# Attention, Sinkhorn gate and eight experts on one core: the opening reordered with the mask formed by GpSimd, and expert 1's leftover pieces dealt out over four slots

## The chip, the core and the metric

The kernel runs on one NeuronCore of a Trainium2 chip. A core has five engines that run their own instruction streams side by side: TensorE (PE in the profile; its weight loads are PEld), VectorE (DVE), ScalarE (ACT), GpSimd (POOL) and SyncE (SP). DMAs are issued from the streams of POOL, ACT and SP and move data on their own; an engine waits for another, or for a DMA, by semaphores. The metric is the device time of one execution in microseconds (us), as the median of several runs.

## The reference

Global-local attention over 8 batches and 8 heads of width 64, with 512 local and 32 global tokens per batch, and then a mixture of experts over the 8 x 544 = 4352 tokens of width 512. Cut to what matters:

```python
# attention, scale = 1/sqrt(64)
k_all, v_all = concat(k_g, k_l), concat(v_g, v_l)
out_g = softmax(scale * q_g @ k_all.T) @ v_all               # global queries see all
mask  = abs(pos[:, None] - pos[None, :]) <= 32               # local ones a band, and the globals
s_ll  = where(mask, scale * q_l @ k_l.T, -1e9)
out_l = softmax(concat(scale * q_l @ k_g.T, s_ll)) @ concat(v_g, v_l)
x = concat(out_g, out_l) as [4352, 512]
# gate: eight Sinkhorn iterations over a [4352, 8] matrix
P = exp(x @ w_gate - max)
for _ in range(8):
    P /= P.sum(1) + 1e-9;  P /= P.sum(0) + 1e-9;  P *= 4352 / 8
# eight dense experts, every token through each
out = sum over e of P[:, e] * (relu(x @ w1[e]) @ w2[e])      # w1 512x1024, w2 1024x512
```

## The kernel before

All engines' orders are the order in which the program is written: the schedule is manual, and every engine takes its instructions strictly in that order. So a line that is moved in the program moves on every engine that it issues to.

**Opening (L226 to L262).** The first two heads of q and k of batch 0 come as float32 by SP and ACT (L229-231) into a buffer f and are cast by L469. The other six heads come by POOL, four loads for q and four for k (`load_qk`, L149, issued at L161). The mask is a tile of 128 partitions x 3 variants x 160 columns (128 of keys, 32 of globals), added to the scores. Its band is made in DRAM: a row with zeros in its first 65 places and -8e9 behind them (`toep_m`, L142; memsets L232-233) is written out 64 times (`scr_m`, L234) and read back skewed, with a pitch of 255, into the two halves of the middle variant (L240-242); L473-476 copy it to the first and last variants, whose edges they set. Global keys and queries of batches 0 to 3 come as float32 (`load_gf`, L201, issued at L205: keys by ACT, queries by SP behind the mask's reads), are cast on DVE by `cast_g` (L208, L210) and turned by `transpose_g` (L213: PE at L217, DVE copy at L219). Those of batches 4 to 7 are loaded by POOL in slot 6 (`load_g`, L194, issued at L198) and turned at the end of slot 8. `load_v` (L170) loads values: on POOL the global ones to a DRAM copy vg16 (L176), the local ones to va (L177, L180) and a tail of vb (L183), and on SP three copies va to vb, shifted by half a tile (L184-186), which wait for va. `load_vz` (L166, issued at L168) has SP read vg16 into four zero-padded places of vgz. For batch 0 it is called at L548, in slot 0 of the loop. `clear` (L250) sets zeros and ones of the value tiles, for batch 0 on DVE and for batch 1 on POOL.

**Attention loop (L477).** 35 slots s, of which 32 hold a pair of heads each (four slots to a batch). A pair passes through stages in successive slots: `st_A` (L266) turns q and k by PE into PSUM, copies the keys to kTe (L274, DVE) and the queries to qbd (L277, ACT); `st_B` (L279) makes scores (L292, L294), adds the mask and takes the row minimum (L299, DVE) and the exponential (L302, ACT), in three parts; `st_D1` (L305) copies the global part (L308, `Pl`) and turns the rest; `st_D2` (L315) turns more; `st_E` (L332) multiplies by the values va, vb (L343) and vgz (L345). Every second slot `st_G0` (L357) copies two blocks of turned global queries into qgbd (L362, DVE, a pair of copies), and `st_G1` to `st_G4` do the global queries' attention. From slot 6 on, pieces of expert 0 and then 1 are set between these stages: `p_l1` (L429, PE at L436) for the first layer, `p_l2` (L443, PE at L450) for the second. POOL's loads are queued by the slot (L477 ff.); from slot 10 on `sums_load` (L98, issued at L101 or L103) and `sums_form` (L105; four subtractions and additions at L116, result stored at L117) make sums of the later experts' weights on POOL. The gate follows (L423 for the logits, then lines L574 to L626), covered by remaining pieces, the `tail`.

**Experts 2 to 7 (L628 on).** They go by a Strassen-like scheme of seven products. `Slot` (L815) is a quarter of one first-layer tile with products m1 to m7 (PE at L838; copies and relu on ACT and DVE at L849 to L877), `Unit` (L724; PE at L743) the second layer. `token_sum` (L672, DVE at L682) makes the token sums that m6, m7 and m4 read. `run_slot` (L883) sets the order of a slot, with `fill` (L892) inserting leftover pieces of expert 1 while no `Unit` is there. `tail` is a list of (cost, piece); when the experts begin four pieces of expert 1 are left, two `p_l1` and two `p_l2`, and all four are placed in slot 0. `jobs` (L948 ff.) hang weight fetches, loads of stored results (`stored_load`) and their additions (`stored_add`) on slots; a load is issued by the addition three before it.

Of the kernel before, what the change touches and what calls it, by code (L numbers as in the profile page):

```python
# [11 lines left out]
FP32 = mybir.dt.float32  # L12
AF = mybir.ActivationFunctionType
ALU = mybir.AluOpType
# [4 lines left out]
NEG = -8.0e9  # L19
# [4 lines left out]
def kernel(  # L24
# [13 lines left out]
    nc = tc.nc  # L38

    B, H, Sl, Dh = q_l.shape  # L40
# [82 lines left out]
    with ExitStack() as att:  # L123
# [15 lines left out]
        vab = [(att_c.tile([P, NJ, H, VW], FP16, name=f"va{i}"),  # L139
                att_c.tile([P, NJ, H, VW], FP16, name=f"vb{i}")) for i in range(2)]  # L140
        xgn = [att_c.tile([P, D], FP16, name=f"xgn{i}") for i in range(2)]
        LT = 256  # L142
        toep_m = att_wk.tile([HB, LT], FP32, tag="ms")
        scr_m = dscr.tile([HB * LT], FP32)
        vg16 = [dscr.tile([Sg, H, Dh], FP16, name=f"vg16_{b}") for b in range(B)]

        staged = {}
# [73 lines left out]
        def run(steps):  # L221
            for f in steps:
                f()
# [5 lines left out]
        for h in range(2):  # L229
            for t, (src, eng) in enumerate(((q_l, nc.sync), (k_l, nc.scalar))):  # L230
                eng.dma_start(out=fh[t][:, :, h, :], in_=src[0, h].rearrange("(s p) d -> p s d", p=P))
        nc.vector.memset(toep_m, NEG)  # L232
        nc.vector.memset(toep_m[:, 0 : 2 * W + 1], 0.0)
        nc.sync.dma_start(out=scr_m.rearrange("(p l) -> p l", l=LT), in_=toep_m)  # L234
        load_gf(0, "kgs", f0[:, 2, :], (nc.scalar,) * 4)
        run(load_qk(0, 2, H))
        nc.vector.memset(ones_f, 1.0)
        nc.scalar.activation(out=ones_f[:, 0:1], in_=ones_f[:, 0:1], func=AF.Exp, scale=0.0)
        nc.vector.memset(mask[:, :, KW:SW], 0.0)
        for hf in range(2):  # L240
            nc.sync.dma_start(out=mask[HB * hf : HB * (hf + 1), 1, 0:KW],
                              in_=scr_m[0 : HB * (LT - 1)].rearrange("(p l) -> p l", l=LT - 1)[:, 0:KW])
        load_gf(0, "qgs", f0[:, 3, :], (nc.sync,) * 4)
        for t in qbd:
            nc.vector.memset(t, 0.0)
        for t in kTe:
# [11 lines left out]
            eng.memset(qgbd[i], 0.0)  # L258

        clear(0, nc.vector)  # L260
        run(load_v(0))
        clear(1, nc.gpsimd)  # L262

        st = {}
# [1 line left out]
        def st_A(n):  # L266
            b, hp = divmod(n, HP)
            qs, ks = staged[b]
            qb, kt = qbd[n % 2], kTe[n % 4]
            pt = ps_tr.tile([P, 2, Sl], FP16, tag="tr")  # L270
            for t, src in enumerate((ks, qs)):
                for so in range(NJ):
                    nc.tensor.transpose(pt[:, t, P * so : P * (so + 1)], src[:, so, 2 * hp : 2 * hp + 2, :], identity)  # L273
            nc.vector.tensor_copy(out=kt[:, W : W + Sl], in_=pt[:, 0, :])  # L274
            for a in range(2):
                r = slice(HB * a, HB * (a + 1))
                nc.scalar.copy(out=qb[r, :, HB * a : HB * (a + 1)], in_=pt[r, 1, :].rearrange("p (i q) -> p i q", q=HB))  # L277
# [189 lines left out]
        NU = B * HP  # L467
        for t in range(2):
            (nc.vector.tensor_copy if t else nc.scalar.copy)(out=staged[0][t][:, :, 0:2, :], in_=fh[t])  # L469
        cast_g("kgs")  # L470
        st_A(0)
        transpose_g(0, "kgs")
        nc.vector.tensor_copy(out=mask[:, 0, 0:KW], in_=mask[:, 1, 0:KW])  # L473
        nc.vector.tensor_copy(out=mask[:, 2, 0:KW], in_=mask[:, 1, 0:KW])
# [2 lines left out]
        for s in range(NU + 3):  # L477
# [57 lines left out]
            f2("a")  # L535
            if g_odd:
                st_G2(gb, gg)
            if 1 <= s:
                st_D2(s - 1 if s <= NU else None, s - 3 if s >= 3 else None)
            if s < NU:  # L540
                st_B(s, 1)
            if 2 <= s < NU + 2 and even:
                st_E(s - 2, 0)
# [1 line left out]
            if s + 1 < NU:  # L545
                st_A(s + 1)
            if s == 0:
                load_vz(0)  # L548
                cast_g("qgs")
                transpose_g(0, "qgs")  # L550
            if s == 1:
# [81 lines left out]
    with tc.tile_pool(name="tpool", bufs=2) as tpool, \  # L633
# [249 lines left out]
        def run_slot(a, jobs=()):  # L883
            p, x = state["slot"], state["unit"]
            y = units.pop(0) if units else None

            def do(who, *what):
                for w in what:
                    if who is not None:
                        getattr(who, w)()  # L890

            def fill(w):  # L892
                while a is not None and tail and w > 0:
                    w -= tail[0][0]
                    tail.pop(0)[1](pool=ps_z, tag="z")

            do(a, "m1")
            if x is None:
                fill(1)
            do(x, "m4", "m5", "r2", "r7")  # L900
            do(a, "m2")
            do(p, "m4", "m3")
            do(y, "sums", "m1")
            if y is None:
                fill(1)
            do(a, "m6")
            do(x, "m3", "r1")
            do(a, "m5")
            if y is None:
                fill(1)  # L910
            do(y, "m7", "m2", "m6")
            do(a, "m7")
            for j in jobs:
                j()
            do(a, "c22")
            state["slot"], state["unit"] = a, y
# [30 lines left out]
        for k, (pas, e) in enumerate(stages):  # L947
            more = k + 1 < len(stages)  # L948
            slots = ([(NQ, 0)] if pas else []) + [(2 * pas + j, f) for j in range(2) for f in range(HF)]
            jobs = [[] for _ in slots]  # L950
            n = len(slots)
            if more:
                jobs[0 if k else 4].append(lambda: fetch(k + 1, 0))
                jobs[5].append(lambda: fetch(k + 1, 1))
            else:
                jobs[5].append(lambda: work.__setitem__("last", load_w2(e)))
            if e == 2 and pas:
                for i in range(4):
                    jobs[1 + i].append(lambda i=i: token_sum(3, i))
            if e == E - 1 and not pas:  # L960
                for i in range(4):
                    jobs[4 + i].append(lambda i=i: token_sum(2, i))
                    jobs[4 + i].append(lambda i=i: token_sum(NQ, i))
            if e == 2:
                us = [(m, c) for q in (([NQ] if pas else []) + [2 * pas, 2 * pas + 1])
                      for m, c1, c2 in ([(B, 0, 1)] if q == NQ else [(2 * q + i, cc, 2 + cc) for i in range(2) for cc in range(2)])
                      for c in (c1, c2)]
                jobs[2].append(lambda us=us: (yq.extend((ee, m, c) for u in range(0, len(us), 2) for ee in range(2)
                                                        for m, c in us[u : u + 2]),
                                              [stored_load() for _ in range(3)]))  # L970
            for i in range(n):
                if e == 2 and i > 4 or e == 3 and i < 5:
                    jobs[i] += [stored_add, stored_add]
                elif 2 < e < E - 1:
                    jobs[i].append(stored_add)
            for (q, f), js in zip(slots, jobs):
                if k == 0 and q == 1 and f == 0:
                    hset.append([hpool.tile([P, FT, 512], FP16, tag="hT", name="hs") for _ in range(2)])
                run_slot(Slot(k, q, f, hset[q % 2] if q < NQ else hg), js)
                if q == NQ or f == HF - 1:  # L980
                    push(k, q)
# [34 lines left out]
```

## Time and profile before

| | |
|---|---|
| median of 3 runs | 1042.97 us (1042.85 to 1044.25) |
| the profiled execution | 1043.23 us, of which the span of its records is 1041.4 |
| mean granted clock of TensorE | 0.998 |
| PE busy | 997.6 us, 96% of the span |
| DVE, ACT, POOL busy | 808.3 (78%), 652.0 (63%), 292.3 (28%) |
| instructions | 20377 |
| opening, the first two of forty slices of 26 us | PE busy 4 and 7 tenths |

The profile comes from one execution. Its page has the busy time of each engine, the span in 40 slices with a busy digit for each engine, the chain of work that ended last, followed back from the end, and the costliest groups of instructions. The trace behind it answers narrower questions: a timeline lists instructions as start, duration, engine, line, operation, output<-input, and in brackets the idle time just before and what ended it; "x2" joins two of a kind in a row, and the duration is then that of both. A list of waits gives, by engine and line, what was waited for: total, times, longest. A row of windows gives a stretch, its length, then busy time (and count) of PE, PEld, DVE, ACT and POOL, the granted clock, the share of the DMA engines and GB/s. Landing of a DMA means the time at which its completion was signalled.

### The profile page before, as it was taken

What the parts mean: (1) busy time and instruction counts of PE and PEld (TensorE: products, weight loads), DVE (VectorE), ACT (ScalarE), POOL (GpSimd) and SP (SyncE); (2) the same over time, 40 slices, a digit from 0 to 9 for tenths busy, and PEclk for the clock granted to TensorE, in tenths of its full rate; (3) what the DMA queues carried; (4) which work ended last, traced back from release to release, by engine and by line L of the source; (5) the groups of instructions that cost most, each with busy time, mean ns of one, the idle gap of its engine ahead of it and who ended that gap; (6) DMA issues with size and microseconds to landing.
All of it is one profiled execution on the core that took longest, in us unless ns stands there. A gap on an engine that the chain in (4) does not pass through costs nothing.

```text
span 1041.4 us, 20377 instructions
## 1 busy us (share of the span) xinstructions
PE 997.6 (96%) x7786; PEld 656.3 (63%) x7786; DVE 808.3 (78%) x2025; ACT 652.0 (63%) x1377; POOL 292.3 (28%) x309
## 2 busy tenths in 40 slices
PE   4789999999999998999999999999999999999998
PEld 3666666566665454666666666676767676676764
DVE  6786766677765554779999888898789999888885
ACT  5787778777785446775555555556765555555551
POOL 9556665656545422002111111111111111011000
PEclk9999999999999999999999999999999999999999
DMA  9999999999975689255463433456554433333043
GB/s 150 183 161 163 184 186 178 166 177 184 183 165 162 182 211 243 62 152 128 110 135 87 112 65 86 90 165 172 154 119 102 108 103 90 68 71 72 1 102 122
DMA packets 184274, 139.42 MB, mean 134 GB/s; under 512 B 120240, under 2 KB 157552, under 8 KB 180592
## 3 DMA queue, kind: packets, MB, share of 16 engines
q0 software_dynamic: 151904, 87.32, 55.0%
q1 hardware_dynamic: 30128, 50.27, 14.7%
q8 instruction: 61, 1.00, 0.4%
q10 hardware_dynamic: 2144, 0.52, 0.3%
q14 instruction: 37, 0.30, 0.1%
HBM read 144.26 MB, written 39.65 MB: 177 GB/s over the span
## 4 chain that ended last, share of the span: by engine, by line
PE 88%; DVE 5%; DMA 3%; ACT 2%; issue 1%; SPq 0%; DVEq 0%; ACTq 0%
PE z L743 27%; PE pa L838 16%; PE ph L436 11%; PE py L450 10%; PE pb L838 8%; PE pc L838 5%; DMA ys<-yd 2%; PE zp L809 1%; PE sc L292 1%; PE po L343 1%; PE po L345 1%; PE pt L273 1%; PE ptw L311 1%; DVE ms L299 1%; PE sg L372 1%
## 5 line engine op out<-in xcount | busy, mean ns | idle before, releaser
L743 PEld LDWEIGHTS <-hs 128*128 128x128 f16 x2264 | 220.7, 98 | 92.9 <-issue 1.1
L743 PE MATMUL z<-w2e,hs 128*128 128x256 f16 x1304 | 195.6, 273 | 0.9 <-DVE oy L777 0.9
L743 PE MATMUL z<-v,hs 128*128 128x256 f16 x960 | 144.0, 273 | 0.0
L436 PE MATMUL ph<-xT,w1e 128*128 128x512 f16 (+1 forms) x576 | 134.0, 367 | 3.1 <-DVE lg L425 3.1
L450 PE MATMUL py<-w2e,hT 128*128 128x512 f16 x544 | 127.4, 379 | 0.8 <-ACT hT L439 0.8
L838 PEld LDWEIGHTS <-w1e 128*128 128x128 f16 x960 | 86.5, 97 | 61.0 <-issue 4.3
L764 ACT COPY z<-z 128x256 f32<-128x256 f32 x98 | 35.0, 357 | 141.9 <-PE z L743 141.9
L838 PE MATMUL pa<-t,s 128*128 128x512 f16 x384 | 114.2, 379 | 0.8 <-ACT s L863 0.8
L299 DVE CUSTOM_DVE_ANT_0 ms<-sc,mask 128x160 f32<-128x160 f32 x256 | 70.1, 321 | 47.8 <-PE sc L294 46.3
L777 DVE SCALAR_TENSOR_TENSOR oy<-z,lg,oy 128x512 f32<-128x512 f32 x128 | 95.8, 749 | 7.3 <-ACT oy L782 4.4
L739 DVE TENSOR_TENSOR hs<-hs 128x512 f16<-128x512 f16 x224 | 94.8, 423 | 8.1
L302 ACT ACTIVATE Pu<-ms,mx 128x160 f16<-128x160 f32 x256 | 92.2, 426 | 8.2 <-DVE mx L299 6.5
L842 DVE CUSTOM_DVE_ANT_0 hx<-pb,s 128x512 f16<-128x512 f32 x96 | 65.9, 686 | 34.7 <-ACT s L872 28.2
L659 POOL DMA_DIRECT2D w1e<-in_moe_w_dram x24 | 17.4, 730 | 268.5 <-PE pa L838 221.4
L854 ACT ACTIVATE hs<-pc 128x512 f16<-128x512 f32 x96 | 57.2, 596 | 53.7 <-PE pc L838 53.6
L659 POOL DMA_DIRECT2D w2e<-in_moe_w_dram x24 | 19.8, 831 | 241.4 <-PE z L743 238.5
L838 PEld LDWEIGHTS <-s 128*128 128x128 f16 x720 | 65.6, 98 | 34.4 <-issue 6.0
L842 DVE CUSTOM_DVE_ANT_0 hs<-pb,s 128x512 f16<-128x512 f32 x96 | 65.9, 686 | 27.1 <-ACT s L872 26.6
L450 PEld LDWEIGHTS <-hT 128*128 128x128 f16 x544 | 51.2, 98 | 51.8 <-issue 1.2
L436 PEld LDWEIGHTS <-w1e 128*128 128x128 f16 x576 | 52.5, 98 | 45.3 <-issue 3.6
L116 POOL TENSOR_TENSOR psum<-pw 128x1024 f16<-128x1024 f16 x24 | 50.4, 2117 | 104.8 <-DMA pw<-in_moe_w_dram 104.8
L453 ACT COPY yst<-py 128x512 f32<-128x512 f32 x68 | 39.9, 586 | 54.4 <-PE py L450 51.9
(186 smaller groups left out, 2053.3 us busy)
## 6 DMA issues: line engine op xcount, KB each, us to landing
ys<-yd SPq DMA_DIRECT2D x68, 256.0 KB, 3.2
yd<-yst SPq DMA_DIRECT2D x16, 1024.0 KB, 4.4
pw<-in_moe_w_dram POOLq DMA_DIRECT2D x12, 1024.0 KB, 11.3
kept<-psum POOLq DMA_DIRECT2D x12, 1024.0 KB, 4.7
s<-kept POOLq DMA_DIRECT2D x12, 768.0 KB, 9.4
v<-kept POOLq DMA_DIRECT2D x12, 768.0 KB, 9.1
w1e<-in_moe_w_dram POOLq DMA_DIRECT2D x12, 512.0 KB, 5.4
w2e<-in_moe_w_dram POOLq DMA_DIRECT2D x12, 512.0 KB, 6.3
```

The lines of the kernel that those rows point to most:

```text
L116: nc.gpsimd.tensor_tensor(out=o, in0=x, in1=y, op=op)
L299: nc.vector.tensor_tensor_reduce(out=ms[:, ii, :], in0=sc[:, SW * ii : SW * (ii + 1)], in1=mask[:, mi, :], scale=-scale, scalar=BIG, op0=A ...
L302: nc.scalar.activation(out=d["Pu"][:, i, :], in_=ms[:, ii, :], func=AF.Exp, scale=-1.0, bias=d["mx"][:, i : i + 1])
L436: nc.tensor.matmul(ph[:, 0:n], wts[e][0][:, dk, P * fm : P * (fm + 1)], xT[:, dk, c0 : c0 + n], start=(dk == 0), stop=(dk == DP - 1))
L450: nc.tensor.matmul(py, hT[:, fk, P * c : P * (c + 1)], wts[e][1][:, fk, :], start=(fk == 0), stop=(fk == FT - 1))
L453: nc.scalar.copy(out=ys[:, c, :], in_=py)
L739: nc.vector.tensor_tensor(out=o, in0=x, in1=y, op=op)
L743: nc.tensor.matmul(o, lhs[:, fk, :], rhs[:, fk, :], start=(first and fk == 0), stop=(fk == HF - 1), skip_group_check=True)
L777: nc.vector.scalar_tensor_tensor(out=o, in0=z, scalar=p, in1=o, op0=ALU.mult, op1=ALU.add)
L838: nc.tensor.matmul(o, lhs[:, dk, P * f : P * (f + 1)], rhs[:, dk], start=(first and n == 0 and dk == 0), stop=(dk == HD - 1), skip_group_c ...
L842: nc.vector._custom_dve(TENSOR_ADD_SAT, out=self.to(i, j), in0=self.of(ps), in1=self.of(s), s0=BIG, s1=0.0)
L854: nc.scalar.activation(out=self.to(0, 0), in_=self.of(self.pc), func=AF.Relu)
```

## The change

The mask's band is formed in place: the whole mask is zeroed on DVE, and for each half of the partitions two GpSimd selects set -8e9 where the column is left of p or right of p + 64; the row, the DRAM copy and its three DMAs go. The loads of global keys are split between SP and ACT, and those of global queries are issued before `load_qk`'s POOL loads and no longer behind the mask's reads. `load_vz(0)` goes from slot 0 of the loop to just behind the first step of `load_v(0)`, so on SP it stands ahead of the copies va to vb. `st_A(0)` goes ahead of the cast of the global keys. For slots 2 to 6 the copy to kTe is made by ACT. In slots 0 to 6 the second part of the scores goes ahead of `st_D2`. In the expert part `fill` counts pieces rather than cost: `some` is the leftover count divided by the slots left of this quarter, rounded up, so the four leftovers of expert 1 go one to each of the first four slots; and for expert 2 the doubled `stored_add` begins at slot 6 and no longer at slot 5.

```diff
@@ -139,9 +139,6 @@
         vab = [(att_c.tile([P, NJ, H, VW], FP16, name=f"va{i}"),
                 att_c.tile([P, NJ, H, VW], FP16, name=f"vb{i}")) for i in range(2)]
         xgn = [att_c.tile([P, D], FP16, name=f"xgn{i}") for i in range(2)]
-        LT = 256
-        toep_m = att_wk.tile([HB, LT], FP32, tag="ms")
-        scr_m = dscr.tile([HB * LT], FP32)
         vg16 = [dscr.tile([Sg, H, Dh], FP16, name=f"vg16_{b}") for b in range(B)]
 
         staged = {}
@@ -229,18 +226,12 @@
         for h in range(2):
             for t, (src, eng) in enumerate(((q_l, nc.sync), (k_l, nc.scalar))):
                 eng.dma_start(out=fh[t][:, :, h, :], in_=src[0, h].rearrange("(s p) d -> p s d", p=P))
-        nc.vector.memset(toep_m, NEG)
-        nc.vector.memset(toep_m[:, 0 : 2 * W + 1], 0.0)
-        nc.sync.dma_start(out=scr_m.rearrange("(p l) -> p l", l=LT), in_=toep_m)
-        load_gf(0, "kgs", f0[:, 2, :], (nc.scalar,) * 4)
+        load_gf(0, "kgs", f0[:, 2, :], (nc.sync, nc.scalar, nc.sync, nc.scalar))
+        load_gf(0, "qgs", f0[:, 3, :], (nc.sync,) * 4)
         run(load_qk(0, 2, H))
         nc.vector.memset(ones_f, 1.0)
         nc.scalar.activation(out=ones_f[:, 0:1], in_=ones_f[:, 0:1], func=AF.Exp, scale=0.0)
-        nc.vector.memset(mask[:, :, KW:SW], 0.0)
-        for hf in range(2):
-            nc.sync.dma_start(out=mask[HB * hf : HB * (hf + 1), 1, 0:KW],
-                              in_=scr_m[0 : HB * (LT - 1)].rearrange("(p l) -> p l", l=LT - 1)[:, 0:KW])
-        load_gf(0, "qgs", f0[:, 3, :], (nc.sync,) * 4)
+        nc.vector.memset(mask, 0.0)
         for t in qbd:
             nc.vector.memset(t, 0.0)
         for t in kTe:
@@ -258,7 +249,15 @@
             eng.memset(qgbd[i], 0.0)
 
         clear(0, nc.vector)
-        run(load_v(0))
+        for a in range(2):
+            band = mask[HB * a : HB * (a + 1), 1, 0:KW]
+            for base, m, c in ((0, -1, 1), (2 * W, 1, -1)):
+                nc.gpsimd.affine_select(out=band, in_=band, compare_op=ALU.is_ge, fill=NEG, base=base,
+                                        pattern=[[c, KW]], channel_multiplier=m)
+        steps = load_v(0)
+        steps[0]()
+        load_vz(0)
+        run(steps[1:])
         clear(1, nc.gpsimd)
 
         st = {}
@@ -271,7 +270,7 @@
             for t, src in enumerate((ks, qs)):
                 for so in range(NJ):
                     nc.tensor.transpose(pt[:, t, P * so : P * (so + 1)], src[:, so, 2 * hp : 2 * hp + 2, :], identity)
-            nc.vector.tensor_copy(out=kt[:, W : W + Sl], in_=pt[:, 0, :])
+            (nc.scalar.copy if 1 < n < 7 else nc.vector.tensor_copy)(out=kt[:, W : W + Sl], in_=pt[:, 0, :])
             for a in range(2):
                 r = slice(HB * a, HB * (a + 1))
                 nc.scalar.copy(out=qb[r, :, HB * a : HB * (a + 1)], in_=pt[r, 1, :].rearrange("p (i q) -> p i q", q=HB))
@@ -467,8 +466,8 @@
         NU = B * HP
         for t in range(2):
             (nc.vector.tensor_copy if t else nc.scalar.copy)(out=staged[0][t][:, :, 0:2, :], in_=fh[t])
+        st_A(0)
         cast_g("kgs")
-        st_A(0)
         transpose_g(0, "kgs")
         nc.vector.tensor_copy(out=mask[:, 0, 0:KW], in_=mask[:, 1, 0:KW])
         nc.vector.tensor_copy(out=mask[:, 2, 0:KW], in_=mask[:, 1, 0:KW])
@@ -535,9 +534,11 @@
             f2("a")
             if g_odd:
                 st_G2(gb, gg)
+            if s < 7:
+                st_B(s, 1)
             if 1 <= s:
                 st_D2(s - 1 if s <= NU else None, s - 3 if s >= 3 else None)
-            if s < NU:
+            if 7 <= s < NU:
                 st_B(s, 1)
             if 2 <= s < NU + 2 and even:
                 st_E(s - 2, 0)
@@ -545,7 +546,6 @@
             if s + 1 < NU:
                 st_A(s + 1)
             if s == 0:
-                load_vz(0)
                 cast_g("qgs")
                 transpose_g(0, "qgs")
             if s == 1:
@@ -889,25 +889,23 @@
                     if who is not None:
                         getattr(who, w)()
 
-            def fill(w):
-                while a is not None and tail and w > 0:
-                    w -= tail[0][0]
+            def fill(n):
+                for _ in range(min(n, len(tail)) if a is not None else 0):
                     tail.pop(0)[1](pool=ps_z, tag="z")
 
             do(a, "m1")
+            some = -(-len(tail) // (HF - a.f)) if tail and a is not None else 0
             if x is None:
                 fill(1)
             do(x, "m4", "m5", "r2", "r7")
             do(a, "m2")
             do(p, "m4", "m3")
             do(y, "sums", "m1")
-            if y is None:
-                fill(1)
             do(a, "m6")
             do(x, "m3", "r1")
             do(a, "m5")
             if y is None:
-                fill(1)
+                fill(some - 1)
             do(y, "m7", "m2", "m6")
             do(a, "m7")
             for j in jobs:
@@ -969,7 +967,7 @@
                                                         for m, c in us[u : u + 2]),
                                               [stored_load() for _ in range(3)]))
             for i in range(n):
-                if e == 2 and i > 4 or e == 3 and i < 5:
+                if e == 2 and i > 5 or e == 3 and i < 5:
                     jobs[i] += [stored_add, stored_add]
                 elif 2 < e < E - 1:
                     jobs[i].append(stored_add)
```

## Prediction

> **What bounds the kernel now.** I read the page's slices and its chain first.
>
> ```profile
> PE   4789999999999998999999999999999999999998
> DVE  6786766677765554779999888898789999888885
> PE 88%; DVE 5%; DMA 3%; ACT 2%; issue 1%; SPq 0%; DVEq 0%; ACTq 0%
> ```
>
> A slice is 26 us. TensorE (PE) is 90% busy or more from the fourth slice on, and 88% of the chain is PE. Matmuls are only moved by this change, so it can win only where PE waits: in the opening (slices 1 to 3), and where expert 1's leftovers meet expert 2 (393 to 413 us). Second, the waits of PE from 0 to 80 us (columns: total, times, longest) and PE's timeline there.
>
> ```profile
> PE po L345 <- DMA vgz<-vg: 2.9, 2, 2.2
> PE pt L217 <- ACT qbd L277: 0.7, 1, 0.7
> ```
> ```profile
> 28.65 0.27 PE L345 MATMUL po<-vgz,pg 128*128 128x130 f16 x1 [2.18 <-DMA vgz<-vg]
> ...
> 74.19 0.39 PE L217 MATMUL pt<-identity,kgs 128*128 128x128 f16 x4
> 75.30 0.38 PE L217 MATMUL pt<-identity,qgs 128*128 128x128 f16 x4 [0.72 <-ACT qbd L277]
> ```
>
> PE stands 2.9 us for the padded global values, and at 75.30 turns the second half of the global queries, after which it has no gap to 149 us. Third, GpSimd (POOL), which issues nearly all loads: the query load, then batch 3's values and the first weights for its sums.
>
> ```profile
> 68.98 1.14 POOL L198 DMA_DIRECT2D qgs<-in_q_g_dram  x2 [0.45 <-DMA va<-in_v_l_dram]
> ...
> 78.45 0.79 POOL L177 DMA_DIRECT2D va<-in_v_l_dram  x1 [0.74 <-PE po L343]
> 79.23 1.77 POOL L180 DMA_DIRECT2D va<-in_v_l_dram  x2
> 80.97 0.78 POOL L103 DMA_DIRECT2D pw<-in_moe_w_dram  x1
> ```
>
> Before the first of these every wait is for a load that landed, or stands where one did; by the DMA records the last of the four query loads lands at 73.45, 1.85 us ahead of its use. Fourth, PE's waits from 80 to 393 us: the largest row is a wait on VectorE (DVE), gaps of 0.66 us at 149.22 and 2.44 at 192.11. DVE's and POOL's timelines show what DVE did then:
>
> ```profile
> 146.15 2.12 POOL L116 TENSOR_TENSOR psum<-pw,psum 128x1024 f16<-128x1024 f16 x1
> ...
> 188.93 4.20 POOL L116 TENSOR_TENSOR psum<-pw 128x1024 f16<-128x1024 f16 x2 [10.71 <-DMA pw<-in_moe_w_dram]
> ```
> ```profile
> 147.06 1.44 DVE L362 COPY qgbd<-qgT 64x64 f16<-64x64 f16 x2
> ...
> 189.94 3.23 DVE L362 COPY qgbd<-qgT 64x64 f16<-64x64 f16 x2
> ...
> 213.67 0.36 DVE L362 COPY qgbd<-qgT 64x64 f16<-64x64 f16 x2
> ```
>
> Alone (213.67) the pair takes 0.36. Begun inside POOL's L116, it ends as L116 ends: at 193.17 against 193.13, and at 148.50 against 148.27. So at two places DVE, and PE behind it, is held to POOL's clock.
>
> **Part 1, the mask band.** Goes: two memsets (0.27 and 0.11), a write (SP issue 1.79) and two reads of 64 partitions; SP's 3.3 us wait between them goes too. The reads landed by 10.84, the copies L473-474 ended at 11.5 and the first masked reduction ran at 11.74, but PE's next slot waited for the key load ks, landed 13.09. That cover stays; without it the part would give about 1 us at the first reduction. Comes: a memset of 480 columns for one of 96 (0.14), taken as 0.5 by the element count, beside the input loads; and four selects on POOL ahead of the value loads L176-183, hence ahead of every later POOL load. Nearest rows: the identity's select, 0.29 for 128x128 f16, and one L116 operation, 2.1 for 1024 columns, as bounds with below-nothing excluded since POOL runs them in order. I take 0.34 by the first, which has the same columns in half the bytes: 1.35 us in all (1.2 to 8.4).
>
> **Part 2, k_g on both queues, q_g ahead of load_qk.** k_g's cast began at 8.83 and q_g's at 14.38, 0.1 after its landing and behind the kTe copy that ended 14.31; earlier landings meet the same cover, ks at 13.09. Eight issues of 0.5 us leave SP's and ACT's idle first 10 us. Cost nothing; 0.3 either way if ACT's first copies move.
>
> **Part 3, vgz of batch 0.** Its four SP issues (19.64 to 23.53, landed 26.05 to 30.45) go ahead of the copies va to vb, whose waits for va held them. vg landed at 13.65, so issues from 14 to 16.4 and landings by 18, 7 us ahead of PE's use at 25. The waits of 2.9 us go. vb's three copies come later by at most the four issues' 2.4 us where SP was not waiting for va; L186 was issued at 18.95 after va landed 18.23, so they stay nearly where they were. The four loads' 1024 packets also leave POOL's loads alone at 23 to 30 us (a 1024-packet load takes about 0.85 us of landing time in the rows at 75 to 81 us, 1.0 when crowded): POOL's chain regains about 1.0 of its 1.35.
>
> **Parts 4 to 6, order in slots 0 to 6.** Keys ahead of a cast (0.43, under the ks cover); the kTe copy on ScalarE for five slots: 5 x 0.42 off DVE, which is 87 to 96% busy from 30 to 60 us, 5 x 0.59 onto ACT, 73 to 85% busy; scores ahead of a transposition. Between losing 0.9 (ACT's excess) and gaining 2.1. I take 1.0. With part 3 the lead of PE at slot 8 is 3.9 (2.0 to 5.0).
>
> **What then ends last.** Through 18 to 66 us POOL waits for landed loads and not for PE, so the query load cannot follow the lead. It lands at 73.45 + 0.4 (1.35 - 1.0; -0.3 to +1.2), and PE, with 0.1 us for the semaphore, goes on at 73.95: 75.30 - 73.95 leaves **1.35** of 3.9. Then POOL's clock: the values at 78.45 waited for PE until there; now PE releases at 77.1, but POOL, which was free at 77.71, comes at 77.71 + 0.4 = 78.1. So pw is issued 0.35 earlier, and so are L116 and all that POOL does after it, since from here to 225 us POOL waits only for its own weights. The copy pairs at 147 and 189.9, 1 us earlier against L116, still begin inside the row of L116 operations (139.66 to 148.27), or just before one; held to its end, PE leaves at 148.3 with a lead of **0.35** (POOL's bounds: +1.0 to -0.45). A lead beyond POOL's is given back here.
>
> **Part 7, leftovers of expert 1.** Slots 0 to 3 took 6.69, 4.52, 4.37 and 4.42, 20.0 in all, with the four pieces in slot 0:
>
> ```profile
> 393.45:400.14 6.69, 6.69 (x38) 3.42 (x37) 6.12 (x19) 3.64 (x9) 2.71 (x4) 1.00 0.75 156
> 400.14:404.66 4.52, 3.56 (x17) 1.46 (x16) 1.53 (x3) 3.09 (x6) 2.94 (x4) 1.00 1.00 228
> ```
>
> The second and third numbers are length and PE's busy time: slot 0 has no gap, slots 1 to 3 lose 0.96, 1.03 and 1.08 (row: pa copied to pc by ACT, 0.9 each). One piece per slot covers 2.2 of these 3.1. But in slot 0 PE comes to the first token sums at about 395.3, and DVE finishes them at 396.6 and 396.9 (two of 0.38 from 396.18): 1.3 + 0.13 us, and ACT's 0.45 at m7 and 0.4 elsewhere come on top. 2.3 new against 2.2 gone: **+0.1** (-2.5 if DVE's sums move up, +1.0 if ACT's copies queue).
>
> **Part 8, stored_add one slot later.** The stalls of 1.75 at 452.82 and 755.86 wait for a load issued by an add three earlier; same order, cost nothing; a further 1.75 if the add lands beside another load.
>
> **Sum**, on the profiled execution (1043.23; span 1041.4 and 1.83 around it): 1043.23 - 0.35 + 0.1 = 1042.98. The median of the runs is 0.26 lower: **1042.7**.
>
> **Rivals.** *Lead kept:* DVE's copies slip past L116. At 189.94 the pair began 1.0 us into L116, and 1.35 against 0.35 is a shift of just 1.0; if it slips out, the 2.44 goes as well: 1042.97 - 1.35 - 2.44 + 0.1 = 1039.3. For: that edge. Against: at 147 another L116 lies just ahead (143.95 to 146.08), so the hold takes the lead first. [...]
>
> *Clock drop:* PE now stands some 2.5 us (3.9 - 1.35) before 73.95. At 44 to 46 us PE was busy 0.70 of 2.00, and the granted clock was 0.67 and 0.50 in the next two rows of 2 us. A drop of 3.4 us at half costs up to 1.7. It eats the lead of 1.35 and 0.35 more, by which POOL then waits for PE: 1042.97 + 0.35 + 0.1 = 1043.4. Against: PE was busy right before and after. [...]
>
> *Spread hides all:* DVE's token sums, free of the pieces' copies, are ready when PE comes: the 2.3 falls away and 0.3 more: 1042.7 - 2.6 = 1040.1. Against: the sums began at 396.18 behind the gate's work, which doesn't move.
>
> *Slower, the selects:* each costs t above 1.0 us. POOL is then late by 4t - 1.0, comes to 77.71 with it instead of 78.45, and all L116 with it; at t = 1.2, 3.8 - 0.74 = 3.1 is forced on DVE at 147: 1042.97 + 3.1 + 0.1 = 1046.1. It passes +2.1 from t = 0.96. For: L116's 2.1; against: the 0.29 row.
>
> **How the numbers follow.** Forecast 0.50 (with POOL's +1.0 to -0.45 of lead and the spread's +1.0, 1042.0 to 1044.4), clock drop 0.14, lead kept 0.13, spread 0.12, selects 0.11. What a measurement of this kernel can tell from no change is 0.2%, 2.1 us: 1040.9 to 1045.1. Faster: 0.13 + 0.12 = 0.25; same: 0.50 + 0.14 = 0.64; slower 0.11. The range leaves out the selects (0.11): it runs from 1039.1, the lead kept with 0.2 to spare, to 1045.0, the clock drop (+0.35) with the query load at its late end (0.8 more) and the spread's +1.0.
>
> **What would show it.** Selects near 0.34 each; no vgz wait at 25 to 29 us; PE waiting for qgs at 70 to 74; L116 at 91.4 instead of 91.74; a copy pair near 147 or 190 still ending with L116, with a longer gap of PE behind it; slot 0 near 5.0 with a wait for L682, slots 1 to 3 near 4.7 to 5.2. It is wrong if PE's qgs transposes come before 73.5 (loads followed the lead), or if PE's lead at 200 us is not POOL's.

## The result, and the profile after

The changed kernel takes 1047.36 us (median of 14 runs, 1045.35 to 1051.43) against 1042.94 us for the kernel before (14 runs, 1040.15 to 1046.56); the ratio is 1.0043, 95% interval 1.0029 to 1.0057. It is slower, by 4.4 us, and outside the range of 1039.1 to 1045.0 that was forecast. Timed once more on another chip, with 12 runs against 32, the ratio was 1.0026 (1.0009 to 1.0043). The profiled execution after took 1045.89 us, span 1044.1, against 1043.23 and 1041.4 before; it is the second shortest of its 14, so what follows explains less than the whole 4.4.

A forecast of stages can be checked stage by stage. For each matmul, its start in the changed kernel minus its start in the kernel before is PE's **lag** (below zero: PE is ahead). Along the time of the kernel before it goes:

| at us | 20 | 28 | 52 | 68 | 85 | 132 | 184 | 230 | 290 | 350 | 380 | 424 | 950 |
|---|---|---|---|---|---|---|---|---|---|---|---|---|---|
| lag | -0.7 | -4.7 | -5.6 | -4.48 | +0.90 | +0.90 | +1.68 | +0.76 | -0.07 | +1.25 | +2.44 | +2.46 | +2.56 |

So the opening did win 4.5 us, and lost 5.4 in one place. Two of PE's waits from 0 to 80 us after the change (total, times, longest):

```profile
PE pt L214 <- DMA qgs<-in_q_g_dram: 3.3, 1, 3.3
...
PE pt L214 <- DMA kgs<-in_k_g_dram: 1.3, 1, 1.3
```

L214 is L217 of before. The 2.9 us for vgz are gone; the loads of the second half of the global keys and queries, which are turned at the end of slot 8, have taken their place. PE's timeline at the end of slot 8 after the change, one line of the same in the kernel before, and the windows of the changed kernel around it (length, busy PE, PEld, DVE, ACT, POOL, then the granted clock):

```profile
71.18 0.38 PE L214 MATMUL pt<-identity,kgs 128*128 128x128 f16 x4 [1.30 <-DMA kgs<-in_k_g_dram]
74.83 0.59 PE L214 MATMUL pt<-identity,qgs 128*128 128x128 f16 x4 [3.27 <-DMA qgs<-in_q_g_dram]
75.21 3.10 PE L435 MATMUL ph<-xT,w1e 128*128 128x512 f16 x8
```
```profile
75.52 1.89 PE L436 MATMUL ph<-xT,w1e 128*128 128x512 f16 x8
```
```profile
72.00:74.00 2.00, 0.00 (x0) 0.00 (x0) 0.04 (x1) 0.00 (x0) 2.00 (x4) 1.00 1.18 186
74.00:76.00 2.00, 1.17 (x6) 0.71 (x7) 0.42 (x1) 0.00 (x0) 2.00 (x3) 0.56 1.86 124
76.00:78.00 2.00, 2.00 (x7) 0.78 (x6) 0.00 (x0) 0.60 (x1) 2.00 (x3) 0.59 2.29 153
```

PE waits 1.30 and 3.27 us, and the eight matmuls behind the wait take 3.10 us where before the same eight took 1.89: the granted clock is at 0.56 and 0.59. That is 1.21 us more. GpSimd's timeline has the selects at their forecast price and SyncE's has the loads of vgz early; GpSimd's first sum begins at 90.87, where 91.4 was forecast:

```profile
8.29 1.36 POOL L255 TENSOR_SCALAR_AFFINE_SELECT mask<-mask 64x128 f32<-64x128 f32 x4
...
13.01 2.61 SPq L165 DMA_DIRECT2D vgz<-vg  x4
...
90.87 4.21 POOL L116 TENSOR_TENSOR psum<-pw 128x1024 f16<-128x1024 f16 x2 [3.00 <-DMA pw<-in_moe_w_dram]
```

And the hold of DVE's copies by GpSimd's sums (L116) is there again at both places; DVE's lines come first, POOL's second:

```profile
148.25 1.93 DVE L361 COPY qgbd<-qgT 64x64 f16<-64x64 f16 x2
...
191.62 2.33 DVE L361 COPY qgbd<-qgT 64x64 f16<-64x64 f16 x2
```
```profile
147.84 2.12 POOL L116 TENSOR_TENSOR psum<-pw,psum 128x1024 f16<-128x1024 f16 x1
...
191.79 4.19 POOL L116 TENSOR_TENSOR psum<-pw 128x1024 f16<-128x1024 f16 x2 [11.70 <-DMA pw<-in_moe_w_dram]
```

The first pair ends at 150.18, its L116 at 149.96 (the second copy of the pair follows, 0.17); of the second pair the second copy is held, to 193.95. Through all twelve sums DVE's copies from SBUF (`Pl`, `qgbd`) that begin in an L116 end 0.03 to 0.09 us after that L116.

### The profile page after: what moved, and what is told of

It is laid out like the page before. It is cut to its first block, busy times and chain, and to the rows that moved or that the text cites. A ratio compares the mean times of both kernels' runs of the same rounds, so it can differ in the third digit from the quotient of the medians.

```text
span 1044.1 us, 20383 instructions
## 1 busy us (share of the span) xinstructions
PE 998.3 (96%) x7786; PEld 653.9 (63%) x7786; DVE 806.3 (77%) x2018; ACT 654.2 (63%) x1382; POOL 293.6 (28%) x313
## 4 chain that ended last, share of the span: by engine, by line
PE 86%; DMA 6%; DVE 4%; POOL 2%; ACT 1%; issue 1%; DVEq 0%; ACTq 0%; POOLq 0%
PE z L743 27%; PE pa L838 16%; PE ph L435 10%; PE py L449 10%; PE pb L838 8%; PE pc L838 4%; DMA ys<-yd 2%; DMA w2e<-in_moe_w_dram 2%; DMA va<-in_v_l_dram 1%; PE zp L809 1%; PE sc L291 1%; PE po L342 1%; PE po L344 1%; PE pt L272 1%; PE ptw L310 1%; DMA qs<-in_q_l_dram 1%
## 5 line engine op out<-in xcount | busy, mean ns | idle before, releaser
L116 POOL TENSOR_TENSOR psum<-pw 128x1024 f16<-128x1024 f16 x24 | 50.7, 2126 | 107.5 <-DMA pw<-in_moe_w_dram 107.5
L438 ACT ACTIVATE hT<-ph 128x512 f16<-128x512 f32 (+1 forms) x115 | 65.1, 568 | 17.8 <-PE ph L435 16.8
```

Source lines behind the costliest of these rows:

```text
L116: nc.gpsimd.tensor_tensor(out=o, in0=x, in1=y, op=op)
L438: nc.scalar.activation(out=hT[:, fm, 0:n], in_=ph[:, 0:n], func=AF.Relu)
```

## The experiments

Thirteen kernels, each timed in five rounds beside the kernel before on the same chip. That kernel's own median was 1044.2 to 1045.7 on those chips, with single runs from 1039.8 to 1051.0, so only ratios are compared. Lags are against the one profile of before. Where the opening is untouched, the lag at 68 us was still +0.80 in the first kernel, +1.5 in the seventh and -0.74 in the tenth: a lag means something only from about 1.5 us on.

| kernel | ratio (95%) | lag at 68 | 85 | 184 | 350 | 380 | 950 |
|---|---|---|---|---|---|---|---|
| 1 before, spread alone | 0.9993 (0.9975 to 1.0011) | +0.80 | +0.79 | +1.99 | +4.57 | +4.78 | +4.42 |
| 2 change without spread | 0.9999 (0.998 to 1.0018) | -5.20 | +1.13 | +2.08 | +2.17 | +3.66 | +3.78 |
| 3 change, globals loaded early | 0.997 (0.9951 to 0.9989) | -4.42 | -4.43 | -0.73 | -2.56 | -1.18 | -1.20 |
| 4 before, copies on ACT | 1.001 (0.999 to 1.003) | +5.85 | +6.99 | +7.17 | +3.92 | +7.82 | +6.46 |
| 5 whole change again | 1.0026 (1.0009 to 1.0043) | -3.55 | +2.80 | +3.08 | +3.79 | +9.92 | +10.07 |
| 6 change, late turning | 0.9974 (0.9957 to 0.9991) | -4.64 | -5.91 | -3.69 | -4.39 | -2.59 | -2.64 |
| 7 before, copies on ACT from slot 8 | 0.9978 (0.9964 to 0.9992) | +1.50 | +1.50 | +1.63 | -1.55 | +0.22 | -1.04 |
| 8 = 6 with the copies of 7 | 0.9951 (0.9935 to 0.9967) | -5.07 | -6.26 | -5.68 | -6.01 | -1.69 | -0.55 |
| 9 = 8 with sums two slots earlier | 1.0021 (1.0002 to 1.004) | -5.10 | -6.37 | -5.80 | +3.02 | +3.02 | +0.74 |
| 10 before, sums two slots earlier | 1.0066 (1.0043 to 1.0088) | -0.74 | -0.73 | +3.05 | +10.12 | +10.12 | +8.72 |
| 11 before, values early, late turning | 0.9971 (0.9951 to 0.9991) | -3.88 | -5.09 | -4.85 | -4.33 | -2.74 | -3.13 |
| 12 before, mask alone | 1.0002 (0.9982 to 1.0023) | -0.17 | -0.16 | +0.82 | +1.93 | +2.80 | +2.37 |
| 13 = 11 with the copies of 7 | 0.9939 (0.9919 to 0.9959) | -2.62 | -3.90 | -3.33 | -6.53 | -4.61 | -5.41 |

Where the turning is moved out of slot 8, the lag at 85 us is some 1.2 us lower for that alone: two turnings go, and with them a wait of 0.72 that stood between them in the kernel before. Only 0.45 of it is paid back in slot 10. The kernel before with the late turning and nothing else was not run, so some of what 6, 8, 9, 11 and 13 gain may be this.

**1. Spread alone.** The edits of `run_slot` and `jobs` put into before.

> The kernel before with the last two parts of the change alone: expert 1's four leftover pieces dealt out over slots 0 to 3, and the doubled additions one slot later. Theory A (the loss comes from the opening; the spread is even): within 1 us of before, and matmuls after 415 us late by 0.0 to 0.3. Rival B (the spread costs the loss): 3 to 4.4 us slower than before.

The ratio is even and its interval ends at 1.1 us slower, so rival B is out for the spread by itself; the lag is +4.78 at 380 and +4.81 at 424 us, so the four slots took the same time. The lag of 4.78 is not the spread's: no code before 393 us differs. It is what one execution of the same code differs from another by, most of it in the holds at 195 to 250 us (gaps of PE of 3.32, 0.73, 0.51).

**2. All but the spread.**

> The changed kernel with the four leftover pieces again all in slot 0 and the additions as before, so the opening edits alone. Theory A: 2 to 4.5 us slower than before, as the whole change is. Rival B: within 1 us of before.

In the trace as theory A says: ahead by 5.20, behind by 1.13 after waits of 1.86 and 3.29 us. In time it missed, being even with before (0.9999); on that chip the median of before was 1045.74, and the interval of 0.2% leaves room for 2 us. In the trace it settles the place of the loss, and that the four slots are even without the spread too: +3.66 at 380 us, +3.67 at 424. In time it leaves a gap: both parts of the change are even when run alone, and the whole is 0.26 to 0.43% slower. Whether the two cost something together was not tested; the changed kernel's own trace shows nothing of it (lag +2.44 at 380, +2.46 at 424).

**3. The second half of the globals loaded early.**

```diff
-                if s == 4:
-                    queue += [load_second]
-                if s == 6:
-                    queue += [lambda: load_g(1, "kgs"), lambda: load_g(1, "qgs")]
+                if s == 4:
+                    queue += [lambda: load_g(1, "kgs"), lambda: load_g(1, "qgs"), load_second]
```

> The changed kernel with the second half of the global keys and queries loaded ahead of expert 1's weights rather than behind batch 2's values. Theory A (the lead of 4.5 us is lost in PE's wait for these loads, and 1.2 more in the halved clock after the wait): no wait at either transposition of slot 8, granted clock 1.0 from 70 to 80 us, PE 3.5 to 4.5 us ahead of before at 85 us. What is left at the end then tells two more apart: if VectorE's copies are held to the end of GpSimd's operations and so tie PE to GpSimd's time, the lead is cut back between 99 and 200 us to GpSimd's own, and the time is 1041 to 1043.5; if the holds only shift at random, the lead stays and the time is 1039 to 1041. Rival C (another load, batch 2's or 3's keys, is late at the same place): PE waits there instead and the time stays near 1047.

They landed by 57.15 us; PE does not wait for them (the 0.7 between the two turnings is there as in the kernel before), the clock is at 1.00 from 70 to 80 us, and the lead of 4.43 stays at 85 us. It is faster than before. The holds then take 3.7 of the lead by 184 us; from there on the kernel before loses in its own holds, and 1.2 are left at the end of this profile. So the trace has the lead cut back to GpSimd's time as the first of the two theories says, while the ratio (0.3%, 3.1 us) falls into the range of the second: one profile cannot tell them apart.

**4. The two copies on ScalarE.**

```diff
-            nc.vector.tensor_copy(out=d["Pl"], in_=d["Pu"][:, :, KW:SW])
+            nc.scalar.copy(out=d["Pl"], in_=d["Pu"][:, :, KW:SW])
-                nc.vector.tensor_copy(out=qg[r, :, W * a : W * (a + 1)], in_=qgT[...])
+                nc.scalar.copy(out=qg[r, :, W * a : W * (a + 1)], in_=qgT[...])
```

> The kernel before with the two small copies that are read from SBUF, that of the global part of the probabilities and the pair of the turned global queries, on ScalarE and not on VectorE. Theory H (VectorE is held by GpSimd's two-operand operations while it copies from SBUF, and PE's gaps of 0.66, 2.44, 0.18, 0.30, 0.72 and 0.28 us between 149 and 320 us come of it): these gaps go, 3 to 4.5 us faster than before, 1038.5 to 1040. Rival D (the holds cost PE nothing on the whole, because it then waits elsewhere, or ScalarE, 75 to 85% busy in the loop, becomes the bound by its 0.5 us more in each slot): within 1 us of before, or slower.

Both theories are half right. From 85 to 323 us PE has not one gap over 0.15 us, and gains 3.1. But in slots 0 to 8, where ScalarE is 81% busy in the kernel before (30 to 60 us), the copies wait in its queue: PE waited 8.9 us for `Pl` and 7.1 for `qgbd`, and lost 7.0.

**5. The whole change again.**

> The whole change once more, timed beside the three below. Theory A, with holds that shift from run to run: PE ahead by 4.5 us until the turning of the second half of the global queries, behind by 0.5 to 1.2 us after it, and between 1 us and 4.5 us slower than before at the end, by where the holds fall. Rival E (the first comparison was off by chance and the whole change is even): within 1 us of before.

Slower again, by 2.7 us (0.9 to 4.5), which all but rules out rival E. The lags miss theory A's figures (ahead by 3.55 at 68 us, behind by 2.80 at 85). This profile fell on a long execution (1053.4 us), and shows best where such a one loses: 6.1 us between 350 and 380 us, in the gate. POOL, DVE and PE there:

```profile
365.33 4.40 POOL L116 TENSOR_TENSOR psum<-pw,psum 128x1024 f16<-128x1024 f16 x2
```
```profile
366.05 1.52 DVE L591 TENSOR_SCALAR rs<-rs 128x34 f32<-128x34 f32 x1
367.60 0.37 DVE L592 RECIPROCAL rs<-rs 128x34 f32<-128x34 f32 x1
368.00 2.02 DVE L593 TENSOR_TENSOR lg<-lg,rs 128x272 f32<-128x272 f32 x1
```
```profile
370.75 0.60 PE L600 MATMUL pc<-cp,ones_f 128*128 128x8 f32 x2 [2.87 <-DVE cp L595]
371.19 8.13 PE L449 MATMUL py<-w2e,hT 128*128 128x512 f16 x24
```

The last sum of weights came 7.8 us later than in the profile of before. L591, 0.18 us when free, ends with one L116 and L593, 0.44 when free, with the next. PE runs out of pieces, waits 2.87 us, and comes back at half clock (0.50 from 372 to 376 us): 24 matmuls in 8.13 us.

**6. The turning in slot 10.**

```diff
-            if s == 8:
+            if s == 10:
                 transpose_g(1, "kgs")
```

> The changed kernel with the second half of the global keys and queries turned at the end of slot 10 and not of slot 8; batch 4, which needs them, begins in slot 16. No load is moved. Theory A: no wait for these loads, granted clock 1.0 from 70 to 80 us, PE ahead by 4 to 4.5 us at 85 us, as with the early loads, and 2 to 4 us faster than before at the end. Rival C (the loads behind are late as well): PE waits in slots 8 to 10 for batch 2's values or keys and is less than 2 us ahead at 100 us.

As theory A has it, with no load moved. On the same chip the whole change was at 1.0026 and this kernel, one number different, is at 0.9974: 0.52%, some 5.4 us, as much as the trace of the changed kernel loses at that place. The window that stood at 0.00 PE busy in the changed kernel is full, at full clock:

```profile
72.00:74.00 2.00, 2.00 (x20) 1.18 (x18) 1.95 (x11) 1.44 (x5) 2.00 (x4) 1.00 1.27 197
74.00:76.00 2.00, 2.00 (x25) 1.41 (x24) 1.16 (x7) 1.59 (x4) 2.00 (x4) 1.00 1.78 124
```

**7. The copies on ScalarE from slot 8 on.** As 4, with `(nc.scalar.copy if n > 7 else nc.vector.tensor_copy)`, and `b > 1` for the pair.

> The kernel before with the two small copies from SBUF on ScalarE from slot 8 on only, so that the opening is left as it is. Theory H: no hold of VectorE and no gap of PE over 0.35 us from 85 to 320 us, where before had 4.3 us; 3 to 5 us faster than before. Rival D: PE waits for ScalarE instead in these slots, and the gain stays under 1 us.

PE's waits from 85 to 350 us in this kernel, and after them the same of before, whose two largest rows are gone:

```profile
PE py L450 <- ACT hT L439: 0.8, 2, 0.5
PE pl L423 <- DVE lg L425: 0.3, 1, 0.3
```
```profile
PE ph L436 <- DVE lg L425: 3.1, 2, 2.4
PE tgx L321 <- DVE pw L313: 1.0, 2, 0.7
```

Theory H holds for the gaps; the gain of 0.22% (2.3 us) is a little under its range.

**8. Both.**

> Both: the changed kernel with the turning in slot 10 and with the two copies on ScalarE from slot 8 on. Theories A and H together: the lead of 4 to 4.5 us stays whole from 85 us and grows to 7 to 9 us by 320 us; 6 to 9 us faster than before. If the lead is tied to GpSimd's time in another way than by these copies, it ends near GpSimd's own lead, 0 to 2 us, and the gain is that of the copies alone, 3 to 5 us.

The lead of 6 us is whole at 350 us, but it did not grow to 7 to 9: it had reached 8.0 at 230 us, and a wait of 1.70 for keys at 268 us, in which nothing was held, took most of the 2 back. 4.3 go in the gate, where PE waits 2.49 us. Faster by 0.49%, 5.1 us, under the 6 to 9 expected.

**9 and 10. GpSimd's sums two slots earlier.** `if 8 <= s < 8 + 4 * (E - 2)` for 10, first with 8, then in before alone.

> The kernel of the last experiment (turning in slot 10, the two copies on ScalarE from slot 8) with GpSimd's weight sums begun in slot 8 and not in slot 10. Theory G (what still varies from run to run, and costs 1 to 6 us between 350 and 376 us, is GpSimd's last sums, which hold the gate's VectorE operations; PE runs dry behind them and comes back at half clock): the last of L116 ends before 345 us, no wait of PE over 1 us from 350 to 370 us, the lead of 6 us at 350 us stays; 7 to 9 us faster than before, and the runs lie closer together than the 5 us of the last one. Rival F (the gate's own chain is too long for the pieces that cover it): the same loss at 352 to 376 us, 4 to 6 us faster than before as without it.

> The kernel before with the weight sums begun in slot 8 and nothing else. Theory G: runs above 1045 us become rare, the median 1.5 to 4 us below before. Rival F: within 1 us of before. If the sums, now beside batch 3's loads, delay these, PE waits for keys or values near 100 us and it is slower.

The part on the gate came true: no operation of DVE is held there, and both kernels have the same lag at 350 and 380 us (3.02; 10.12). But POOL's loads of the coming batches now stand behind sums, and PE waits for keys, 7.2 us in the first of the two and 6.5 in the second. Two of these waits in the first:

```profile
229.80 0.23 PE L272 MATMUL pt<-identity,ks 128*128 128x128 f16 x1 [1.41 <-DMA ks<-in_k_l_dram]
230.67 0.23 PE L272 MATMUL pt<-identity,ks 128*128 128x128 f16 x1 [0.64 <-DMA ks<-in_k_l_dram]
```

Both are slower: a wait taken out at the gate came back as a later load. In the second, where the copies are still on VectorE, the earlier sums also meet the pair of copies at 83.71 us, which takes 3.65 us instead of 0.36; PE waits 2.19 behind it, the granted clock falls to 0.50 (90 to 92 us), and the lag goes from -0.73 to +3.26.

**11. The values alone, with the late turning.** `load_vz(0)` early, as in the change, in before.

> The kernel before with the padded global values of batch 0 moved early, as in the change, and with the turning of the second half in slot 10; no select, no other edit of the opening. If the lead of the opening comes from the values (2.9 us of waiting, as predicted): PE 2.5 to 4 us ahead at 64 us and at 85 us, 2 to 3 us faster than before. If it comes from the order of the copies and scores in slots 0 to 6: under 1.5 us ahead, and within 1 us of before.

Ahead by 3.88 at 68 us, and by 2.62 with the same opening in experiment 13, where the seven profiles with the whole opening have 3.55 to 5.20: most of the opening's lead is this one move. 0.29% faster, of which the late turning may have a part. The late query load landed at 72.25.

**12. The mask alone.**

> The kernel before with the mask band formed by GpSimd alone; nothing else is moved. In the runs so far the last of the late query loads landed at 72.9 to 75.0 us with the opening of before, at 72.25 with the values early alone, and at 73.9 to 76.3 with the whole opening of the change. Theory S (the selects hold back all of GpSimd's loads by their own 1.36 us, and that is what the change loses against the values early alone): the landing at 75 to 76.5, PE waits for it in slot 8, PE 0.5 to 2 us late at 85 us, 0.5 to 2.5 us slower than before. Rival T (the later landing comes from the global loads that go ahead, not from the selects): the landing at 73 to 75 as before, no wait, within 1 us of before.

It landed at 74.45, inside what the opening of before shows (72.9 to 75.0), and PE did not wait for it: that meets rival T's conditions, though the landing is 0.6 later than the mean of before. That the global loads are the cause, as T has it, is not shown by this. The selects alone cost nothing that this can measure.

**13. The values, the late turning and the copies.**

> The kernel before with the values early, the turning in slot 10, and the two copies on ScalarE from slot 8: no select, no other edit of the change. If theories A and H hold and add up: PE 4 to 5 us ahead at 85 us, no hold to 320 us, 7 to 8 us ahead there, 1.3 to 6 lost again at the gate; 4 to 7 us faster than before, no slower than the same with the whole change. If the other opening edits are worth their 1 us: slower than that by as much.

Faster than before by 0.61% (6.4 us), the best of all. Its interval overlaps that of 8, on another chip, so no gain of the rest of the change is seen once the waits are out. The lag at 380 us still holds a loss of 1.9 in the gate.

## Why the prediction was wrong, point by point

**Where PE waits, and that the lead is capped: right, and its size short.** The lead of 4.48 at slot 8 (forecast 3.9, 2.0 to 5.0) was indeed cut by the query load, as experiments 3 and 6 show from two sides. The step that failed is in "What then ends last": "It lands at 73.45 + 0.4", and the 1.35 us of lead that this leaves. The load landed at 74.59, and PE went on at 74.83, not 73.95: 0.88 lost. Then the clock, a rival put at 0.14 and left out of the sum: 1.21, where up to 1.7 was allowed (from half clock for 3.41 us, as in the kernel before at 46.66 to 50.07). With the transpositions themselves slower by 0.2, that makes the whole difference between the 1.35 ahead that was forecast and the 0.90 behind that came. The landing itself lies inside the margin that was given for it (73.15 to 74.65); what the sum went by was a lead that one landing in one profile left, where kernels with the same opening differ by 2.1 us in it. The late landing and the clock together were still inside the forecast's range; what takes the profile out of it are the holds below.

**The reason against the clock drop failed.** Against the drop I gave that PE was busy right before and after. It was (1.88 of 2.00 us from 68 to 70, all 2.00 from 76 to 78), and the clock halved all the same. The forecast was one wait of 2.5 us; with the late landing the waits are 1.30 and 3.27, with 0.38 of PE's time between. The runs have the drop after shorter waits too: the clock was halved for some 3.4 us behind waits of 3.32 (experiment 1), 2.49 (8), 2.38 (12), 2.19 (10) and 1.95 (4, at the gate), for twice that behind 2.87 (5), and not behind 2.44 (before, at 192 us), 2.17 (4, slot 8) and 2.08 (3); the last section shows for three of them how they differ. So a single wait of 2.5 would not have ruled the drop out either.

**Why the load is later is not settled.** The landing was 72.9 to 75.0 us in five kernels with the opening of before (mean 73.9), 73.9 to 76.3 in six with the whole new opening and the loads in their old place (mean 75.0), 72.25 and 72.01 with the values early alone, 74.45 with the mask alone. By these few runs the values gave back more than the 1.0 counted, and the selects took 0.6 by one run, less than their 1.36; both are of the size by which one kernel differs from another with the same opening, and what the parts do together does not add up. The global loads moved ahead were not run alone.

**"PE leaves at 148.3 with a lead of 0.35": the tie is right, the time of GpSimd wrong.** At the end of the third sum, L116's own lag and PE's behind it are 1.68 and 1.68 in the changed kernel, 1.99 and 2.00 in experiment 1, 1.94 and 1.95 in 2, 3.02 and 3.02 in 5, 0.83 and 0.83 in 12, and -4.85 and -4.84 in 11. Where the pair falls into an earlier L116 (3 and 6) they part: -0.85 and -3.06, +0.35 and -4.05. But I carried L116's start (forecast 91.4, measured 90.87) on to the third sum as it was; by then it had lost 2.5 us, through landings of weights that differ from run to run. Even the first start was near by luck: its weights were to be issued 0.35 us earlier and were issued 0.90 later (81.87 for 80.97), but landed 8.9 us behind their issue and not 10.7.

**The holds were counted at two places.** The trace of before has eleven held copies up to 320 us, and three operations of the gate, held for 1.67, 1.47 and 1.34 us longer than free; they made no gap of PE there, and so I passed over them. In the changed kernel they took 0.8 up to 150 us, gave back 1.75 up to 290 (there the kernel before lost more), and took 1.25 at 321 and 1.19 at 363 (PE's gaps of 1.09 and 0.92): the lag went from 0.90 to 2.44 where no order of work had changed, with the clock full. The range had no term for these 1.54 us. With a halved clock behind the longer gaps they are the largest part of what one profile differs from another by after the opening: 3.8 us from 85 to 350 us in experiment 1 and 6.1 us at the gate in 5.

**Right as put:** the selects' price (0.34 each), vgz's landings (17.5 to 19.35 for 18) and the wait that goes, the first slots' cover, the additions one slot later, and the spread: slots 0 to 3 even, +0.02 for +0.1, the wait on L682 at 1.1 for 1.3.

**Profile and median.** The profiled execution is 2.7 us over that of before, the medians are 4.4 apart. The other 1.7 are within what the holds vary by from run to run; that they come of the holds is argued, not shown.

## What to carry to other kernels

Before an opening is made faster, look for the next thing that keeps its own time, a load paced by the queue and not by the compute, and ask who stands in order behind its use; here a transposition in slot 8, of data first needed in slot 16, turned 4.5 us won into 0.9 lost. A wait of PE can cost a second time, in the clock behind it: of the waits listed above, six of 1.95 to 3.32 us did, and three of 2.08 to 2.44 did not. Where one engine holds another by overlap, one profile is one draw: compare the gaps of several, and take the hold out rather than tune around it.

## What the runs showed of the hardware

**The hold.** In the traces of the kernel before and of the changed kernel, VectorE's f16 copies from SBUF (`Pl` and `qgbd`, 0.22 and 0.18 us when free) that began while GpSimd ran a two-operand operation (L116) ended with it. All 24 of them (11 and 13) end 0.03 to 0.09 us behind the end of the L116 in which they began, whether they began 0.01 or 1.62 us after its start, and so took 0.58 to 2.15 us. The f32 tensor-scalar L591 ended 0.04 behind in all three cases, and the two-operand operations L593 and L604 0.30 behind in four cases; a fifth, an L604 begun 0.10 us before the end of an L116, took its free 0.44. Other operations that began in an L116 kept their times in these two traces: the reductions L590 (0.44) and L595 (0.64 to 0.65), the reciprocal L592 (0.37), a tensor-scalar of one column (L375, 0.15, four times) and the masked reductions of the scores, which read PSUM (L299, 0.33 at most in 126 cases). A pair of GpSimd's operations took 4.49 us at the most in these traces (before, from 357.41), for 4.20. GpSimd's own issuing of loads went with longer copies too, by less: outside the sums, all 21 copies that took over 0.06 us longer than free (0.50 at the most) began during such an issue and ended between 0.02 us before its end and 0.05 behind it, while 28 others that began during one were not longer than that 0.06. On ScalarE the same copies met no hold: 0.39 to 0.40 and 0.23 to 0.24 for every one from slot 8 to 320 us in experiment 7.

**The clock.** In the traces of the kernel before and of the changed kernel the granted clock changes only at the ends of steps of 3.41 us: 3 steps at full clock, 1 at half and 290 at full before (recorded from 36.42 us on), and 1 at full, 1 at half, 13 at full, 1 at half and 283 at full after the change (from 23.03), with half clock at the end of both. Of these 590 steps at full clock five were followed by half clock: PE was busy in them for 1.54 us (before, from 43.25), 1.48 and 0.38 (after, from 23.03 and 70.82) and, at the end of the two kernels, 1.03 and 0.12. In the other 585 PE was busy for 1.69 us or more. So in these traces it is not the length of a wait alone that tells, but how it lies on the steps. Here are two steps of the kernel before, which share the wait of 2.44, and two of experiment 12, where the wait of 2.38 falls into the first (columns as above):

```profile
190.02:193.43 3.41, 2.09 (x27) 1.28 (x25) 3.33 (x5) 1.55 (x4) 3.33 (x3) 1.00 0.41 77
193.43:196.84 3.41, 2.29 (x16) 1.12 (x15) 2.37 (x7) 1.21 (x3) 3.33 (x2) 1.00 0.43 100
```
```profile
192.22:195.63 3.41, 1.03 (x13) 0.67 (x10) 3.26 (x7) 0.38 (x1) 3.33 (x2) 1.00 0.70 156
195.63:199.05 3.42, 3.42 (x14) 1.32 (x12) 1.17 (x4) 1.41 (x4) 3.04 (x3) 0.50 0.12 19
```

The wait of 2.17 in experiment 4, behind which the clock stayed at 1.00, lies across the end of a step in the same way: counted back from that trace's half stretch of 371.08 to 374.49 us, one ends near 77.5, and PE is busy for 0.00 us of 76 to 78. In the changed kernel the step from 70.82 to 74.23 us has PE busy for 0.38 us, and the next runs at 0.50.
